# A gated recurrence with a soft mixture of experts: PSUM banks shared by need, filler transposes, wide roots and a new order of work

## The chip, the cores and the metric

The kernel runs on one core of a Trainium2 chip. Its engines are TensorE (PE, with its weight loads PEld), VectorE (DVE), ScalarE (ACT) and GpSimd (POOL); SyncE (SP) issues the DMAs. The metric is the device time of one execution in microseconds. A profiled execution lists the span from its first to its last instruction as well.

## The reference

The inputs are x, r_gate and i_gate of shape 4 x 5056 x 256, a_param of 256, phi of 256 x 32, and two weight arrays for eight experts.

```python
log_a = 8.0 * sigmoid(r_gate) * np.log(np.clip(sigmoid(a_param), 1e-6, 1 - 1e-6))
a_t = np.exp(log_a)
norm = np.sqrt(np.maximum(1.0 - a_t * a_t, 1e-6))
x_gated = norm * sigmoid(i_gate) * x
for t in range(S):
    h = a_t[:, t] * h + x_gated[:, t]
    y[:, t] = h
# y becomes 20224 x 256
logits = y @ phi                                   # 20224 x 32
d = softmax over the 20224 tokens of logits
slot_input = d.T @ y                               # 8 experts x 4 slots x 256
slot_out[e] = np.maximum(slot_input[e] @ w1[e], 0) @ w2[e]
c = softmax over the 32 slots of logits
out = c @ slot_out
```

Nothing can be written before all tokens have been read, because d is a softmax over tokens. So the kernel has a first part (recurrence, logits and the running weighted sum), a middle (the experts on 32 slots) and a last part (the second softmax and the output).

## The kernel before, in words

**Tiling.** 512 tokens are a quad (QT); there are 40, the last with 256 tokens. Units (UNITS) are quad 0 alone, then pairs of quads, then quad 39 alone: 21 units. Chunks (CHUNKS) are two units each, ten of them, and a last chunk of one. The 256 features are two halves h of 128. Tokens lie along the free dimension for the scan, so r and the gated x are transposed on TensorE, 128 x 128 at a time, and y is transposed back.

**One quad or unit passes these tasks** (the names are the planner's). TR (line 451) transposes a quad of r into PSUM, and SR (461, ACT) takes the tanh of half of it, which stands for the sigmoid. EX (492, ACT) makes a from it, per unit and half; SQ (503, POOL) squares a into a buffer N. SI (473, ACT) is the sigmoid of i, U (481, POOL) multiplies it with x, both in the natural layout. RT (516, ACT) is the root of 1 - a*a in N. TU (533, PE) transposes U's result into PSUM, ST (547, DVE) multiplies it with the root, SC (564, DVE) is the scan, which writes h over a in the buffer A. TY (584, PE) transposes h back and YC (598 on ACT, 600 on DVE) copies it from PSUM to yn.

**One group of four quads** passes LG (636, PE, logits), LE (649, DVE, with the running maximum), LD (665, POOL), TE (680, PE, transposes), ES (690, ACT, exponential), AC (710, PE, the weighted sum) and AE (726, DVE). After the last group come the merge of the partial sums (852 to 882), L1 (908), HS (922), HT (930), HR (936) and L2 (947) of the experts, and the table for the output (966 to 980). The last part has, per group, CT, CM, CS, CE, RR, CN, CH and CL (1014 to 1052), then HP (1079), HE (1090, 1092), OT (1102), OE (1114, 1116) and the store (1126).

**What sets the order.** Every engine runs its instructions in one fixed order, which a planner in the file works out while the kernel is built. It simulates the five engines from tasks with durations, latencies, dependences, buffers and priorities; at each free moment an engine takes the ready task with the lowest priority number whose buffers are free. ACT differs: its tanh, exponential, sigmoid and root tasks follow a written sequence (act_seq, lines 760 to 801), because a switch between the tables of the functions is an instruction of its own. Each chunk has three phases: tanh and exponentials, sigmoids, roots. PRE quads of the next chunk have their tanh in the sigmoid phase (PRE0 for chunk 0). The loads on SP follow the same sequence: r at each SR, i and x at each SI. A task without a table (a copy) may go ahead of the sequence only if its priority number is below that of the next one by more than ALAG (pick_act, line 246). DVE is asked before ACT when both could take a task.

**Buffers.** In SBUF: st (loaded tiles; 12), A (7), N (4), yn (7). In PSUM, eight banks of 512 floats per partition: rp (one pair of banks, for TR), up (two pairs, for TU; TR may use them as well, SHARE = 1), ms (two single banks). Single banks hold everything else; the halves of rp (tr) may serve as singles after the last tanh, and those of up (tu) after the last scan (tag_after, line 802). A pair for TU is held from TU until the end of SC.

The weights of the experts are loaded into st, A and N buffers as these come free (lines 808 to 836).

Of the kernel before, what the change touches and what calls it, by code (L numbers as in the profile page):

```python
# [15 lines left out]
P = 128  # L16
J = 4
# [7 lines left out]
PRE0 = 2  # L25
YLAG = 3

ALAG = 100
FILL = False
TRP = 2  # L30
# [3 lines left out]
SHARE = 1  # L34
G0 = 1
GM = 1
N_ST = 12
N_A = 7
N_N = 4
# [3 lines left out]
LOAD = 1.283  # L43
# [39 lines left out]
class Planner:  # L83
    def __init__(self, slots):
        self.tasks = []
        self.slots = {t: list(range(n)) for t, n in slots.items()}
        self.act_seq = []

        self.tag_after = {}
# [12 lines left out]
    def run(self):  # L102
# [41 lines left out]
        def begin(t, e):  # L144
            nonlocal n
            for b in t.alloc:
                b.tag = self.tag_for(b)
                b.slot = [self.slots[b.tag].pop(0) for _ in range(b.need.get(b.tag, 1))]
# [13 lines left out]
            for x in t.eng:  # L162
                ready[x].remove(t)
# [6 lines left out]
        while n_done < len(self.tasks):  # L170
# [4 lines left out]
            while finish and finish[0][0] <= now + 1e-9:  # L175
                _, _, t = heapq.heappop(finish)
                n_done += 1
                for b in [*t.alloc, *t.uses]:
                    b.users -= 1
                    if b.users == 0:  # L180
                        self.slots[b.tag] += b.slot
                for o in outs[id(t)]:
# [5 lines left out]
            while again:  # L188
                again = False
                for e in ("DVE", "ACT", "PE", "POOL", "SP"):  # L190
# [31 lines left out]
                    elif cands:  # L222
                        t = min(cands, key=lambda t: t.prio)
                        begin(t, e)
                        again = True
        self.end = now
        return order

    def tag_for(self, b, taken={}):
        for g in b.tags:  # L230
            if any(x.end is None or x.end > self.now + 1e-9 for x in self.tag_after.get(g, ())):
                continue
            if g == "tr" and not self.slots["rp"]:
                continue
            if b.late is not None and not b.late(self, g):
                continue
            if len(self.slots[g]) - taken.get(g, 0) >= b.need.get(g, 1):
                return g
        return None

# [28 lines left out]
def kernel(  # L269
# [37 lines left out]
    def plen(p):  # L307
# [5 lines left out]
         "rp": 1, "up": 2, "ms": 2, "tu": 4, "tr": 2, "hs": 4, "rm": 2, "hT": 2, "bd": 1}  # L313
    )
    T = {}
    if tc is not None:
# [91 lines left out]

    def load(nm, q):
# [13 lines left out]
        ld[(nm, q)] = add("SP", f"D{nm}{q}", 1.30 * n / J, prio=q, emit=emit, alloc=[b])  # L423
# [17 lines left out]
    def mk_sr(q):  # L441
# [3 lines left out]
        rp = Buf(("rp", "up") if SHARE & 1 else "rp", f"rp{q}")  # L445
# [11 lines left out]
        tr = add("PE", f"TR{q}", 0.245 * n, deps=[ld[("r", q)], t_const], prio=q - TRP, emit=e_tr,  # L457
# [28 lines left out]
    def mk_ex(p):  # L486
        c = plen(p)
        for h in range(H):
# [7 lines left out]
            EX[(p, h)] = add("ACT", f"EX{p}.{h}", 0.2 + 0.935 * c / 1024,  # L496
# [13 lines left out]
    def mk_rt(p):  # L510
        c = plen(p)
        for h in range(H):

            def e_rt(h=h):
                v = t(Nb[p])[:, h, :c]
                nc.scalar.activation(v, v, AF.Sqrt, bias=1.0, scale=-1.0)  # L516

            RT[(p, h)] = add("ACT", f"RT{p}.{h}", 0.1 + 0.85 * c / 1024, deps=[SQ[(p, h)]],
                             prio=pos_u(p), emit=e_rt, uses=[Nb[p]], kind="sqrt")

    def mk_scan(p):
        c = plen(p)
        tok0 = quads(p)[0] * QT
        for h in range(H):
            up = Buf(("up", "rp") if SHARE & 2 else "up", f"up{p}.{h}")
            up.late = lambda pl, tag: tag == "up" or SR[NQ - 1].start is None
# [12 lines left out]
            tu = add("PE", f"TU{p}.{h}", 0.123 * c / P, deps=[U[q] for q in quads(p)], prio=pos_u(p) - 20 + h * 0.1,  # L539
# [11 lines left out]
            ST[(p, h)] = add("DVE", f"ST{p}.{h}", 0.06 + 1.065 * c / 1024, deps=[tu, RT[(p, h)]],  # L551
# [21 lines left out]
    def mk_y(q):  # L573
        p, i = unit[q]
        YC[q] = []
        for b0 in range(0, qlen(q) // P, 2):
            yp = Buf(("ms", "tr", "tu"), f"yp{q}.{b0}")
# [24 lines left out]
            yc = add(("DVE", "ACT"), f"YC{q}.{b0}", 0.60 * nb / 2, deps=[ty], prio=q + (YLAG if q < NQ - YEND else 0),  # L602
# [11 lines left out]
    def mk_group(g):  # L614
# [8 lines left out]
        lp = Buf(("ms", "tr", "tu"), f"lp{g}")  # L623
        lD = Buf("lD", f"lD{g}")
        eS = Buf("eS", f"eS{g}")
        ep = Buf(("ms", "tr", "tu"), f"ep{g}")
        acc = Buf(("ms", "tr", "tu"), f"acc{g}")
# [3 lines left out]
        for h in range(H):  # L631

            def e_lg(h=h):
                for j, (q, o, _) in enumerate(segs):
# [8 lines left out]
                     prio=pos - 4 + fin, emit=e_lg, alloc=[] if h else [lp],  # L643
# [61 lines left out]
        for b in range(nb):  # L705

            def e_ac(b=b):
                for j, (q, o, _) in enumerate(segs):
# [10 lines left out]
                     prio=pos - 30 + fin, emit=e_ac, alloc=[] if b else [acc],  # L719
# [445 lines left out]
```

## Time and profile before

| | us |
|---|---|
| median of 3 runs | 337.19 (336.81 to 338.89) |
| the profiled execution | 339.49 |
| its span | 337.7 |
| mean granted TensorE clock over the span | 0.913 |
| HBM read / written | 78.94 MB / 20.71 MB |

The profile gives the busy time of each engine, the same by stretches of the span, groups of instructions by source line, and each engine's instructions in order of time. A row of a stretch has: its limits, its length, busy microseconds of PE, PEld, DVE, ACT and POOL with the count of instructions, the granted clock as a share of full speed, the DMA share and GB/s. A row of the timeline has start, length, engine, line, operation, output<-input, shape and count; several like instructions in a row stand as one row, and the bracket says how long the engine idled before it and what released it. A group has, after the first bar, busy us and mean ns of one instruction, and after the second the idle time before them.

### The profile page before, as it was taken

Reading aid. Unit: us, or ns where it says so; the run is one execution under the profiler, and the core shown is the slowest. Engines: PE = TensorE matmul, PEld = TensorE weight load, DVE = VectorE, ACT = ScalarE, POOL = GpSimd, SP = SyncE. Lnnn points to the kernel's source line nnn. Section 1 sums busy time; section 2 is a strip of 40 time slices with the busy share of each in tenths; the row PEclk is TensorE's granted clock in tenths of the full one; section 3 lists DMA queues with packets and bytes.
Section 4 is the critical chain, followed back from the end, with each engine's and each line's share of the span. In section 5 each row is a group of like instructions: output and inputs, shape, how many; then the busy total and the mean of one; then the engine's idle time right before and its main releaser. Section 6 shows DMA issues by size and latency. Waiting matters only on the chain. (4 is left out here: it accounts for less than half of the span.)

```text
span 337.7 us, 5590 instructions
## 1 busy us (share of the span) xinstructions
PE 266.9 (79%) x2032; PEld 187.3 (55%) x2032; DVE 259.7 (77%) x336; ACT 259.9 (77%) x306; POOL 198.9 (59%) x143
## 2 busy tenths in 40 slices
PE   4467639768789597895986969888889989979981
PEld 3357525644656456564664645754545567656761
DVE  0118847986979999789799999999833599898661
ACT  5977999989989999999799999995200049857650
POOL 4464687969949789698597978942010063375000
PEclk9755958978979999599899999799999999999997
DMA  7999876795876988869688796897995007979996
GB/s 240 416 411 378 284 265 233 276 352 207 328 291 234 364 296 293 304 229 358 222 309 323 268 338 202 310 403 282 376 387 202 3 1 305 397 297 380 406 400 274
DMA packets 30556, 100.02 MB, mean 296 GB/s; under 512 B 3648, under 2 KB 3648, under 8 KB 30528
## 3 DMA queue, kind: packets, MB, share of 16 engines
q1 hardware_dynamic: 29984, 99.63, 79.8%
q8 instruction: 16, 0.26, 0.3%
q10 hardware_dynamic: 544, 0.03, 0.1%
q14 instruction: 12, 0.10, 0.1%
HBM read 78.94 MB, written 20.71 MB: 295 GB/s over the span
## 5 line engine op out<-in xcount | busy, mean ns | idle before, releaser
L503 POOL TENSOR_TENSOR N<-A 128x1024 f32<-128x1024 f32 (+1 forms) x40 | 72.8, 1831 | 49.7 <-ACT A L492 49.4
L481 POOL TENSOR_TENSOR st<-st,st 128x1024 f32<-128x1024 f32 (+1 forms) x39 | 90.7, 2352 | 2.2 <-ACT st L473 2.2
L564 DVE TENSOR_TENSOR_SCAN A<-A,A,up 128x1024 f32<-128x1024 f32 (+4 forms) x40 | 82.2, 2060 | 2.0
L533 PE MATMUL up<-ident,st 128*128 128x128 f32 x316 | 50.6, 312 | 27.0 <-DVE A L564 23.5
L547 DVE SCALAR_TENSOR_TENSOR up<-N,up 128x1024 f32<-128x1024 f32 (+2 forms) x42 | 48.6, 1161 | 29.3 <-PE up L533 14.5
L533 PEld LDWEIGHTS up<-ident,st 128*128 128x128 f32 x316 | 40.7, 160 | 40.5 <-DVE A L564 19.3
L584 PE MATMUL ms<-ident,A 128*128 128x128 f32 x296 | 43.8, 285 | 10.4 <-DVE yn L600 8.9
L492 ACT ACTIVATE A<-A,ca 128x1024 f32<-128x1024 f32 (+2 forms) x42 | 48.9, 1184 | 0.5
L600 DVE COPY yn<-ms 128x512 f32<-128x512 f32 x67 | 43.3, 678 | 2.6 <-PE ms L584 2.5
L584 PEld LDWEIGHTS ms<-ident,A 128*128 128x128 f32 x296 | 33.6, 144 | 20.0 <-DVE yn L600 14.8
L473 ACT ACTIVATE st<-st 128x1024 f32<-128x1024 f32 (+1 forms) x40 | 39.6, 1037 | 0.1
L516 ACT ACTIVATE N<-N 128x1024 f32<-128x1024 f32 (+2 forms) x42 | 38.9, 995 | 0.1
L451 PE MATMUL rp<-ident,st 128*128 128x128 f32 x172 | 28.1, 315 | 12.9 <-DMA st<-in_r_gate_dram 9.4
L451 PEld LDWEIGHTS rp<-ident,st 128*128 128x128 f32 x172 | 23.3, 164 | 19.2 <-issue 5.7
L1045 POOL TENSOR_TENSOR lS<-lS,rs_all 128x512 f32<-128x512 f32 (+2 forms) x11 | 10.6, 962 | 31.9 <-DVE rs_all L1037 26.2
L1102 PE MATMUL ms<-bd,hT 128*128 128x512 f32 x88 | 27.8, 420 | 2.0 <-DVE st L1116 0.8
L461 ACT ACTIVATE A<-rp 128x1024 f32<-128x1024 f32 (+1 forms) x22 | 21.7, 987 | 5.0 <-PE rp L451 5.0
L710 PE MATMUL ms<-yn,eS 128*32 128x257 f32 x284 | 24.6, 396 | 0.4 <-ACT eS L690 0.4
L1031 ACT ACTIVATE lS<-lS 128x512 f32<-128x512 f32 (+2 forms) x11 | 6.4, 589 | 23.9 <-DVE lS L1028 23.6
L451 PE MATMUL up<-ident,st 128*128 128x128 f32 x144 | 20.2, 287 | 5.6 <-DVE A L564 4.9
L1114 ACT COPY st<-ms 128x512 f32<-128x512 f32 x28 | 16.3, 591 | 10.0 <-PE ms L1102 9.2
L636 PE MATMUL ms<-A,phi_sb 128*32 128x512 f32 x136 | 22.8, 700 | 0.3 <-ACT yn L598 0.3
(133 smaller groups left out, 397.5 us busy)
## 6 DMA issues: line engine op xcount, KB each, us to landing
st<-in_i_gate_dram SPq DMA_DIRECT2D x39, 512.0 KB, 5.3
st<-in_x_dram SPq DMA_DIRECT2D x39, 512.0 KB, 5.2
st<-in_r_gate_dram SPq DMA_DIRECT2D x38, 512.0 KB, 4.9
out_dram<-st SPq DMA_DIRECT2D x38, 512.0 KB, 3.6
A<-in_moe_w_dram SPq DMA_DIRECT2D x16, 512.0 KB, 5.6
st<-in_moe_w_dram SPq DMA_DIRECT2D x10, 512.0 KB, 6.1
N<-in_moe_w_dram SPq DMA_DIRECT2D x6, 512.0 KB, 7.8
st<-in_r_gate_dram SPq DMA_DIRECT2D x3, 256.0 KB, 3.2
```

Of the source, the lines that this page charges most:

```text
L451: nc.tensor.transpose(out=o[:, m, :], in_=t(st[("r", q)])[:, m * D + h * P : m * D + (h + 1) * P], identity=ident,)
L473: nc.scalar.activation(v, v, AF.Sigmoid)
L481: eng.tensor_tensor(out=v, in0=t(st[("i", q)])[:, : n * D], in1=v, op=ALU.mult)
L492: nc.scalar.activation(v, v, AF.Exp, scale=ca[:, h : h + 1], bias=ca[:, h : h + 1])
L503: eng.tensor_tensor(out=t(Nb[p])[:, h, :c], in0=v, in1=v, op=ALU.mult)
L516: nc.scalar.activation(v, v, AF.Sqrt, bias=1.0, scale=-1.0)
L533: nc.tensor.transpose(out=o[:, m, :], in_=t(st[("x", q)])[:, m * D + h * P : m * D + (h + 1) * P], identity=ident,)
L547: nc.vector.scalar_tensor_tensor(v, t(Nb[p])[:, h, :c], 1e-3, v, op0=ALU.max, op1=ALU.mult)
L564: nc.vector.tensor_tensor_scan(dst, dst, flat()[:, s0:s1], init, op0=ALU.mult, op1=ALU.add)
L584: nc.tensor.transpose(out=t(yp)[:, b * D + h * P : b * D + (h + 1) * P], in_=t(A[p])[:, h, o : o + P], identity=ident,)
L600: nc.vector.tensor_copy(out=dst, in_=v)
L1102: nc.tensor.matmul(t(op), t(hT)[:, b * P // 2 : (b + 2) * P // 2], T["bd"][part].rearrange("p i d -> p (i d)"), start=(part == 0), stop=(p ...
```

## The change

1. PSUM. The tags rp, up, ms, tu and tr are gone. All eight banks are four pairs (tag pair) whose halves are singles (tag one). TR and TU take a pair, at most RPM = 2 for r and UPM = 2 for x at a time. Everything else takes a single: first the free half of a pair already broken, else a half of the highest free pair, as long as fewer than ONEP = 3 pairs are broken (4 after the last scan has begun).
2. Filler. From 4 to 60 us of the plan, where TensorE has no task that can run, at least three banks are free and one has been free for over 1 us, two transposes of the identity into that bank are put in.
3. Roots. For the second unit of every chunk (WIDE) one ACTIVATE over both halves takes the place of two.
4. Order. No tanh of chunk 1 in chunk 0's sigmoid phase (PRE0 2 to 0). Priorities: TR at q - 10 (was q - 2), TU at pos - 28 (was - 20), LG at pos - 10 (was - 4), TY at q + 8 (was q + 2), YC at q + 7 (was q + 3). ALAG 100 to 0. A few assumed durations and latencies of the planner are changed.
5. Buffers: st 12 to 10, A 7 to 9, N 4 to 3; the bytes are the same.

```diff
-PRE0 = 2
-YLAG = 3
-ALAG = 100
+PRE0 = 0
+YLAG = 9
+ALAG = 0
-TRP = 2
+TRP = 10
-SHARE = 1
-G0 = 1
+RPM = 2
+UPM = 2
+ONEP = 3
+WARMT = 60.0
+QL = 99
+TUP = 28
+ACP = 30
+LGP = 10
+YCP = -2
+WD = 1
+G0 = 2
-N_ST = 12
-N_A = 7
-N_N = 4
+N_ST = 10
+N_A = 9
+N_N = 3
-LOAD = 1.283
+LOAD = 1.41
...
-            lat = {"PE": 0.25, "ACT": 0.1, "DVE": 0.1, "POOL": 0.12, "SP": 2.0}[eng[0]]
+            lat = {"PE": 0.25, "ACT": 0.13, "DVE": 0.13, "POOL": 0.12, "SP": 2.6}[eng[0]]
...
+                    elif e == "PE" and self.warm is not None and self.warm_from <= now < self.warm_to:
+                        t = self.filler(now)
+                        if t is not None:
+                            begin(t, e)
...
+            if g == "pair":
+                k = b.name[:2]
+                if self.pairs_of.get(k, 0) < self.pair_max.get(k, 4) and any(
+                    {2 * i, 2 * i + 1} <= self.banks for i in range(4)
+                ):
+                    return g
+            elif g == "one":
+                if self.pick_one() is not None:
+                    return g
...
+    def pick_one(self):
+
+        half = [i for i in self.banks if i ^ 1 not in self.banks and i // 2 in self.broken]
+        if half:
+            return min(half)
+        whole = [i for i in range(3, -1, -1) if {2 * i, 2 * i + 1} <= self.banks]
+        if whole and len(self.broken) < self.one_pairs():
+            return 2 * whole[0]
+        return None
+
+    def filler(self, now):
+
+        free = [i for i in self.banks if now - self.since.get(i, -1e9) > 1.0]
+        if len(self.banks) < 3 or not free:
+            return None
+        i = min(free, key=lambda i: self.since.get(i, -1e9))
+        return Task(("PE",), "WU", 0.22, 0.2, (), 1e9, lambda: self.warm(i), alloc=[self.fixed(i)], kind="warm", shape="T")
...
-        make("rp", 1, [P, 2, QT], ps)
-        make("up", 2, [P, 2, QT], ps)
-        make("ms", 2, [P, QT], ps)
+        make("pair", 4, [P, 2, QT], ps)
-        T["tu"] = [T["up"][i // 2][:, i % 2, :] for i in range(4)]
-        T["tr"] = [T["rp"][0][:, i, :] for i in range(2)]
+        T["one"] = [T["pair"][i // 2][:, i % 2, :] for i in range(8)]
...
+    WIDE = {p for ch in chunks for p in ch[WD:]} if WD is not None else set()
...
-        rp = Buf(("rp", "up") if SHARE & 1 else "rp", f"rp{q}")
+        rp = Buf("pair", f"rp{q}")
...
-        for h in range(H):
+        wide = p in WIDE
+        for h in range(1 if wide else H):
 
             def e_rt(h=h):
-                v = t(Nb[p])[:, h, :c]
+                v = t(Nb[p])[:, :, :c] if wide else t(Nb[p])[:, h, :c]
                 nc.scalar.activation(v, v, AF.Sqrt, bias=1.0, scale=-1.0)
...
-            up = Buf(("up", "rp") if SHARE & 2 else "up", f"up{p}.{h}")
-            up.late = lambda pl, tag: tag == "up" or SR[NQ - 1].start is None
+            up = Buf("pair", f"up{p}.{h}")
...
-            yp = Buf(("ms", "tr", "tu"), f"yp{q}.{b0}")
+            yp = Buf("one", f"yp{q}.{b0}")
...
-            yc = add(("DVE", "ACT"), f"YC{q}.{b0}", 0.60 * nb / 2, deps=[ty], prio=q + (YLAG if q < NQ - YEND else 0),
+            yc = add(("DVE", "ACT"), f"YC{q}.{b0}", 0.60 * nb / 2, deps=[ty], prio=q + YCP + (YLAG if q < NQ - YEND else 0),
...
+    def e_warm(i):
+        for _ in range(2):
+            nc.tensor.transpose(out=T["one"][i][:, :P], in_=ident, identity=ident)
+
+    planner.warm, planner.warm_from, planner.warm_to = e_warm, 4.0, WARMT
+    planner.pair_max = {"rp": RPM, "up": UPM}
+    planner.one_pairs = lambda: ONEP if SC[(NP - 1, H - 1)].start is None else 4
```

More of the change, by code (lines that the diff above doesn't have):

```diff
@@ L146, in begin @@
             for b in t.alloc:
[L147 to L148 removed]
+                self.take(b)
             dur = t.alt.get(e, t.dur)
@@ new lines, in give @@
+    def give(self, b):
+        if b.tag == "pair":
+            i = b.slot[0]
+            self.banks |= {2 * i, 2 * i + 1}
+            self.since[2 * i] = self.since[2 * i + 1] = self.now
+            self.pairs_of[b.name[:2]] -= 1
+        elif b.tag == "one":
+            i = b.slot[0]
+            self.banks.add(i)
+            self.since[i] = self.now
+            if i ^ 1 in self.banks:
+                self.broken.discard(i // 2)
+        else:
+            self.slots[b.tag] += b.slot
@@ L762, with roots @@
     ahead = []
+    def roots(k):
+        return [("RT", p, h) for p in chunks[k] for h in range(1 if p in WIDE else H)]
     for k in range(NC):
@@ L776 @@
             phases.append([("SR", q) for q in ahead])
-        phases.append([("RT", p, h) for p in chunks[k] for h in range(H)])
+        if k >= QL and k > 0:
+            phases.append(roots(k - 1) if k > QL else [])
+        if k < QL or k == NC - 1:
+            phases.append(roots(k))
     for ph in phases:
```

95 lines of the change are left out of this document (61 added, 34 removed).

## The prediction

> **What bounds the kernel now.** I read the page first, then busy time by stretches of the span, then the ScalarE instructions in order of time, then who released each pause.
>
> ```profile
> span 337.7 us, 5590 instructions
> ...
> PE 266.9 (79%) x2032; PEld 187.3 (55%) x2032; DVE 259.7 (77%) x336; ACT 259.9 (77%) x306; POOL 198.9 (59%) x143
> ```
> ```profile
> 0.00:20.00 20.00, 9.04 (x41) 7.67 (x42) 3.50 (x7) 14.96 (x16) 9.60 (x33) 0.83 0.90 340
> 20.00:40.00 20.00, 14.86 (x86) 13.44 (x85) 12.94 (x12) 15.72 (x16) 9.95 (x6) 0.66 0.97 361
> ...
> 180.00:200.00 20.00, 16.01 (x145) 11.39 (x145) 19.22 (x21) 19.86 (x22) 17.13 (x9) 1.00 0.84 299
> ```
> ```profile
> 200.00:226.00 26.00, 21.51 (x192) 15.38 (x196) 24.79 (x24) 25.81 (x29) 20.49 (x13) 0.93 0.82 302
> 226.00:241.00 15.00, 12.96 (x111) 7.21 (x104) 14.68 (x19) 6.93 (x14) 2.44 (x2) 1.00 0.90 330
> ...
> 251.00:277.00 26.00, 25.15 (x318) 15.56 (x306) 15.08 (x38) 3.54 (x7) 5.12 (x5) 1.00 0.27 101
> 277.00:332.00 55.00, 50.35 (x235) 34.78 (x235) 45.90 (x87) 36.84 (x68) 18.40 (x18) 1.00 0.90 356
> ```
>
> The averages (ACT and DVE 77%, PE 79%) hide four stages. In a stretch the columns after the length are PE, PEld, DVE, ACT, POOL, then granted clock, DMA share and GB/s. Up to 226 us ACT is the bound: 19.86 of 20 us in the steady part, with DVE close behind at 19.22. From 226 to 241 DVE finishes the scans (14.68 of 15). From 251 to 277 the expert layers run on PE (25.15 of 26), and then the output runs on PE too (50.35 of 55) with the DMA at 0.90. So what is won before 226 moves everything behind it, unless DVE is late; what is won on PE before 226 counts only where ACT waits for it.
>
> ACT's own timeline shows its pace and where it pauses (start, length, and in brackets the pause before):
>
> ```profile
> 14.31 1.28 ACT L473 ACT_TABLE_LOAD   x1
> ...
> 21.91 1.02 ACT L461 ACTIVATE A<-rp 128x1024 f32<-128x1024 f32 x1 [2.44 <-PE rp L451]
> ...
> 24.25 3.04 ACT L516 ACTIVATE N<-N 128x512 f32<-128x512 f32 x4
> 27.31 1.28 ACT L492 ACT_TABLE_LOAD   x1
> ...
> 34.13 1.02 ACT L461 ACTIVATE A<-rp 128x1024 f32<-128x1024 f32 x1 [2.25 <-PE rp L451]
> ...
> 37.58 1.28 ACT L473 ACT_TABLE_LOAD   x1
> ...
> 45.91 3.90 ACT L516 ACTIVATE N<-N 128x1024 f32<-128x1024 f32 x4
> ...
> 74.63 0.60 ACT L690 ACTIVATE eS<-ms 128x512 f32<-128x512 f32 x1 [1.20 <-PE ms L680]
> ...
> 96.98 0.60 ACT L690 ACTIVATE eS<-ms 128x512 f32<-128x512 f32 x1 [1.41 <-PE ms L680]
> ...
> 129.91 1.28 ACT L516 ACT_TABLE_LOAD   x1
> ...
> 145.00 2.01 ACT L473 ACTIVATE st<-st 128x1024 f32<-128x1024 f32 x2
> ...
> 150.74 1.28 ACT L516 ACT_TABLE_LOAD   x1
> ...
> 162.95 0.60 ACT L690 ACTIVATE eS<-ms 128x512 f32<-128x512 f32 x1 [2.22 <-PE ms L680]
> ...
> 173.92 1.28 ACT L516 ACT_TABLE_LOAD   x1
> ```
>
> From one load of the root table to the next an undisturbed chunk takes 150.74 - 129.91 = 20.83 us; the one with the 2.22 us pause takes 23.18. The pauses that can be removed are few: 2.44 and 2.25 us at the start, for the transposed r tiles (L451), and 1.20 + 1.41 + 2.22 = 4.83 us later, where the exponentials of a group (L690) wait for their transposes (L680). Apart from the waits for the first loads, the rest is ACT's own work.
>
> **Part by part: the start (PRE0 = 0).** Two tanh of chunk 1 (L461) leave the sigmoid phase of chunk 0, and their two r loads move behind i2 and x2. Before, this phase held both, with the 2.44 us wait. After, I rebuild it from the rows: sigmoid table at 14.31 as now (1.28 each table), three sigmoids in 2.95, root table, the roots in 3.04 less 0.10: chunk 0 is through at about 22.8 instead of 27.31. Chunk 1's exponential phase now lasts 37.58 - 27.31 = 10.27, minus the 2.25 us wait (its r tiles are transposed while ACT does the roots), plus two tanh at 0.95: 9.9. It ends at 32.7 instead of 37.6. The gain is 4.7 us, the two waits; the moved tanh only change place. Cover: 23 tiles of 512 KB must be in for chunk 1, 12.06 MB; at 340 GB/s and then 361 (rows above) that takes 34.6 us, and the last sigmoid needs its tile at about 37.8. So it fits with some 3 us, and nothing beyond it. Ends: 1.5 (loads late) and 4.7; I take 4.0, as the first two rates are measured with the same queue.
>
> **The second unit's root in one instruction.** The two sizes of root, and a chunk's last squares on POOL:
>
> ```profile
> L516 ACT ACTIVATE N<-N 128x1024 f32<-128x1024 f32 x38 | 37.1, 1046 | 0.1
> ...
> L516 ACT ACTIVATE N<-N 128x512 f32<-128x512 f32 x2 | 1.2, 622 | 0.0
> ```
> ```profile
> 142.63 3.75 POOL L503 TENSOR_TENSOR N<-A 128x1024 f32<-128x1024 f32 x2 [0.77 <-ACT A L492]
> ```
>
> Four roots in a row take 3.90 us (row at 45.91); one alone takes 1.046, so each further one adds 0.951. From 512 to 1024 elements the mean grows from 622 to 1046 ns, 0.848 us per 1024:
>
> One start-up less saves 0.951 - 0.848 = 0.10 us; ten chunks, 1.0 us on the bounding engine. It now waits for both squares of POOL and gives DVE its first half 0.85 us later. Both are covered: the squares end at 142.63 + 3.75 = 146.4, the root runs after 152, and DVE has about 7 us of the first unit's scans before it. Without that cover, 0.85 per chunk.
>
> **PSUM by pairs or singly, and TensorE's new order.** Now r's transposes borrow the banks of the scans, and the queue stands behind a transpose that waits for a scan:
>
> ```profile
> 160.09 1.97 PE L533 MATMUL up<-ident,st 128*128 128x128 f32 x8 [1.60 <-DVE A L564]
> 161.85 1.06 PE L680 MATMUL ms<-ident,lD 128*128 128x128 f32 x4
> ```
>
> That is the 2.22 us pause: L680 is queued behind L533, which waited 1.60 for a scan. UPM = 2 leaves as many scan pairs as now, so this order can come back; but r has two pairs of its own, and logits come forward (LGP). No row prices the new order. Bounds: 0 and 4.83 us of these pauses; I take half, 2.4.
>
> **Filler transposes up to 60 us.** What eight transposes cost at a low and at a full clock stands in a stretch where TensorE did nothing else:
>
> ```profile
> 30.91 1.91 PE L584 MATMUL ms<-ident,A 128*128 128x128 f32 x8
> ...
> 35.21 1.09 PE L451 MATMUL rp<-ident,st 128*128 128x128 f32 x8 [1.11 <-ACT A L461]
> ```
>
> A filler is two transposes: with 8 in 1.09 to 1.97, it takes 0.27 to 0.49 us. It goes where the plan has PE idle, so at worst it stands before a real transpose: with the 11 tanh inputs of that time, up to 5.4 us lost if all are hit, 0 if none. It may raise the clock (0.66 in 20:40): a tanh input's 8 transposes would take 1.09 rather than 1.91, but the two waits this could shorten are already counted. I take -0.3.
>
> Here eight transposes went from 1.91 to 1.09 us within 5 us. The Trainium skill, page "TensorE: Matmul & The Clock Gate", section "Part 4: PE-mode transpose", says the opposite: the full clock does not engage for transpose mode. By that page the fillers would only cost; these rows disagree with it, and by them fillers can warm. As the benefit is counted at nothing, the sum is the same less at most 0.3.
>
> **Copies of y (ALAG 0, YLAG 9, YCP -2).** One copy on either engine:
>
> ```profile
> L600 DVE COPY yn<-ms 128x512 f32<-128x512 f32 x67 | 43.3, 678 | 2.6 <-PE ms L584 2.5
> ...
> L598 ACT COPY yn<-ms 128x512 f32<-128x512 f32 x7 | 3.9, 583 | 3.7 <-PE ms L584 3.7
> ```
>
> A copy that lies some 7 quads behind ACT's next instruction may now go ahead of it on ACT. On DVE it costs 678 ns, on ACT 583, of which 0.10 overlaps as with the roots, so 0.48 us. Before the last root every such copy lengthens the bound; after it, ACT is idle (6.93 of 15) and it is free. Scans now go ahead of copies, so copies do fall behind. Ends 0 and 30 copies (three a chunk); I take 2, -1.0. At the end this order helps: DVE did copies ahead of the last full chunk's first scan product, whose transposes had ended before:
>
> ```profile
> 216.82 2.40 PE L533 MATMUL up<-ident,st 128*128 128x128 f32 x16
> ```
> ```profile
> 220.31 1.22 DVE L547 SCALAR_TENSOR_TENSOR up<-N,up 128x1024 f32<-128x1024 f32 x1
> ```
>
> The transposes of both halves ended at 216.82 + 2.40 = 219.2, the first half at about 218, so scans could start up to 2.3 us earlier. The copies come back later, partly on ACT. Ends -2 and +2.3; I take +1.0.
>
> **Buffers.** Issues of loads, the use of one, and the time to landing:
>
> ```profile
> 123.33 0.37 SPq L421 DMA_DIRECT2D st<-in_i_gate_dram  x1
> ...
> 138.61 7.54 SPq L421 DMA_DIRECT2D st<-in_r_gate_dram  x3
> ```
> ```profile
> 148.47 1.09 PE L451 MATMUL up<-ident,st 128*128 128x128 f32 x8 [0.39 <-DVE A L564]
> ```
> ```profile
> st<-in_r_gate_dram SPq DMA_DIRECT2D x38, 512.0 KB, 4.9
> ```
>
> st 12 to 10: the sigmoid at 145.00 uses the tile issued at 123.33, and r issued at 138.61 is transposed at 148.47. Twelve tiles a chunk make 1.74 us a tile, so two slots less means loads 3.5 us later. Landing takes 4.9 us. So r keeps 9.9 - 4.9 - 3.5 = 1.5 us, i far more. N 4 to 3: the second unit's square must now wait for the root product of the unit two before:
>
> ```profile
> 204.02 1.23 DVE L547 SCALAR_TENSOR_TENSOR up<-N,up 128x1024 f32<-128x1024 f32 x1
> ```
> ```profile
> 207.00 3.75 POOL L503 TENSOR_TENSOR N<-A 128x1024 f32<-128x1024 f32 x2 [0.29 <-ACT A L492]
> ```
>
> Margin 207.00 - 205.25 = 1.75 us, and behind it POOL's products for x. A from 7 to 9 pays for later copies. I take 0 for all three, with up to 1 us a chunk lost if the margins go. G0 changes nothing at GM = 1. The tail after 241 has the same eight banks and engines at work; 0, within 2 either way.
>
> **Sum.** 4.0 + 1.0 + 2.4 - 0.3 - 1.0 + 1.0 = 7.1 us. The profiled execution took 339.49 us (337.7 span and 1.8 around it) and would take 332.4; the median shown is 337.19, so I predict **330.1**.
>
> **Rivals.** (a) *Only the start and the roots pay*: the group pauses return, since L680 still stands behind a waiting scan transpose, and copies and fillers cost their 1.3; end order 0. 4.0 + 1.0 - 1.3 = 3.7 gained: 333.5. For it: the cap of two scan pairs; against: r's own pairs.
> (b) *Loads bind*: with ten slots and r 1.5 us from being late, r waits appear; 0.5 us a chunk over ten eats 5.0: 335.1. For it: DMA share 0.97 in 20:40; against: 299 GB/s suffices later. The Trainium skill's page "DMA: Bandwidth & Descriptors", section "Specifications", puts a core's HBM limit near 358 GB/s; the rows' 361 is no less.
> (c) *Slower: copies on ACT.* DVE is full with 19.22 of 20, scans go first, and ACT takes three copies a chunk: 30 x 0.48 = 14.4 lost against 8.1 gained: 343.5. It decides from 17 copies before the last root on. For it: the copy goes before ACT's own next instruction; against: the 7 quads are nearly two chunks, which a copy seldom waits.
> (d) *More*: all pauses vanish, 4.7 + 1.0 + 4.8 + 2.3 and the tail 2: 14.8, 322.4.
> That sharing banks changes nothing is inside (a).
>
> **How the numbers follow.** Forecast 0.42 (326 to 333), (a) 0.18, (b) 0.15, (c) 0.13, (d) 0.12. A measurement tells about 1% (3.4 us) from no change, so faster means under 333.8: the forecast, (d), and two thirds of (a): 0.66. Same: (b), the rest of (a), the mild end of (c): 0.22. Slower 0.12. The range 322.5 to 338.5 leaves out the far half of (d) and most of (c).
>
> **What would show it.** Right: ACT's exponential table load for chunk 1 near 23 and the sigmoid load near 33; the 42 root instructions become 32, wide ones of about 1.9 us; the L680 pauses halved; chunk pace 20.7. Wrong: more than 17 copies on ACT before its last root; new pauses of ACT behind DMA or of POOL's squares behind DVE; first output later than 273 us.

## The result and the profile after

The changed kernel takes 365.16 us (median of 4 runs, 364.08 to 365.99) against 337.0 for the kernel before (4 runs, 332.88 to 338.89): a ratio of 1.0878, 95% interval 1.0775 to 1.0982. I had forecast 330.1 with an upper end of 338.5, so the sign is wrong and the time lies far above that. Medians in this text are of all executions, ratios leave out the slow ones (some per cent longer at a lower granted clock), and the profile of e10 is of a slow one.

The head of the page after, and the busy time by stretches of its stages (columns as in the prediction: length, PE, PEld, DVE, ACT, POOL, granted clock, DMA share, GB/s):

```profile
span 363.8 us, 5797 instructions
...
PE 280.8 (77%) x2132; PEld 196.7 (54%) x2132; DVE 258.4 (71%) x333; ACT 259.4 (71%) x299; POOL 198.7 (55%) x143
```
```profile
60.00:220.00 160.00, 129.15 (x1054) 93.24 (x1055) 143.54 (x147) 147.18 (x144) 126.69 (x66) 0.90 0.78 282
...
228.00:242.00 14.00, 11.40 (x106) 5.75 (x98) 10.66 (x15) 6.36 (x13) 2.44 (x2) 1.00 0.92 323
242.00:253.00 11.00, 8.55 (x71) 4.34 (x69) 6.23 (x17) 1.41 (x4) 1.05 (x2) 1.00 0.87 327
253.00:283.00 30.00, 25.20 (x315) 14.65 (x316) 13.10 (x34) 2.83 (x7) 4.64 (x4) 1.00 0.33 122
283.00:360.00 77.00, 57.52 (x231) 37.52 (x230) 41.83 (x83) 38.50 (x72) 18.63 (x18) 0.93 0.65 259
```

Read the last row against that of before, where 277 to 332 had PE at 50.35 of 55 and the DMA at 0.90. Now the output takes 77 us, PE is idle for 19 of them and the DMA is at 0.65: nothing is full. Where no engine is full and work remains, the time goes into waits between the engines.

Dates from the timelines of the profiled executions place the loss (us):

| | before | after | longer by |
|---|---|---|---|
| last root of the chunks ends | 226.5 | 228.3 | 1.8 |
| last scan ends (from there) | 241.0 (14.5) | 241.7 (13.3) | -1.2 |
| first expert's first matmul | 250.6 (9.6) | 253.1 (11.5) | 1.8 |
| first output matmul | 277.2 (26.5) | 282.8 (29.7) | 3.2 |
| end of the span | 337.7 (60.6) | 363.8 (81.0) | 20.4 |

The steps are summed to 26.0 of 26.1 us. Almost all of it lies behind the last scan, where I had put 0.

**The start came out as forecast.** ScalarE's timeline (start, length):

```profile
14.35 1.28 ACT L557 ACT_TABLE_LOAD   x1
...
18.61 1.28 ACT L601 ACT_TABLE_LOAD   x1
...
22.87 1.28 ACT L545 ACT_TABLE_LOAD   x1
...
32.94 1.28 ACT L557 ACT_TABLE_LOAD   x1
```

The exponential table of chunk 1 comes at 22.87 (forecast 22.8) and its sigmoid table at 32.94 (32.7). **So did the roots**, in ScalarE's groups by shape:

```profile
L601 ACT ACTIVATE N<-N 128x2048 f32<-128x2048 f32 x10 | 19.0, 1896 | 0.0
L601 ACT ACTIVATE N<-N 128x1024 f32<-128x1024 f32 x18 | 18.1, 1052 | 0.1
```

Ten wide ones of 1.896 us, 32 in all with the four short ones. **The group pauses did not.** ScalarE's groups in 60 to 220 us:

```profile
L775 ACT ACTIVATE eS<-pair 128x512 f32<-128x512 f32 x7 | 4.2, 597 | 11.4 <-PE pair L765 11.4
```

11.4 us of pauses against the 4.83 counted in the prediction. One of them, from all engines in order of time:

```profile
107.51 2.35 DVE L632 SCALAR_TENSOR_TENSOR pair<-N,pair 128x1024 f32<-128x1024 f32 x2
...
109.77 4.58 DVE L649 TENSOR_TENSOR_SCAN A<-A,A,pair 128x1024 f32<-128x1024 f32 x2
...
112.26 1.94 PE L618 MATMUL pair<-ident,st 128*128 128x128 f32 x8 [3.52 <-DVE A L649]
...
114.12 1.94 PE L721 MATMUL pair<-A,phi_sb 128*32 128x512 f32 x8
...
115.99 1.12 PE L765 MATMUL pair<-ident,lD 128*128 128x128 f32 x4
...
117.14 0.60 ACT L775 ACTIVATE eS<-pair 128x512 f32<-128x512 f32 x1 [2.99 <-PE pair L765]
```

TensorE stands 3.52 us at the state transposes L618 until the first scan, which ran behind two state products, has freed a pair. The logits L721 and the group's transposes L765 queue behind it, and ScalarE's exponential is 2.99 us late.

**The output is a chain through the halves of a pair.** All engines in order of time, from the middle of the output (matmuls L1200; the copies of a block on DVE, L1214, and on ACT, L1212):

```profile
341.49 1.19 PE L1200 MATMUL pair<-bd,hT 128*128 128x512 f32 x4 [0.48 <-ACT st L1212]
...
342.72 0.69 DVE L1214 COPY st<-pair 128x512 f32<-128x512 f32 x1 [0.98 <-PE pair L1200]
...
343.44 0.58 ACT L1212 COPY st<-pair 128x512 f32<-128x512 f32 x1 [1.03 <-DVE st L1214]
344.08 1.20 PE L1200 MATMUL pair<-bd,hT 128*128 128x512 f32 x4 [0.90 <-ACT st L1212]
```

PE fills both halves of a pair, DVE copies one half, ACT copies the other only when DVE has done, PE goes on only when ACT has done: 344.08 - 341.49 = 2.59 us for these two blocks, and of the three steps on them no two overlap. The waits in 283 to 360 us (total, times, longest) show the same:

```profile
PEld pair L1200 <- ACT st L1212: 15.4, 15, 1.9
...
ACT st L1212 <- DVE st L1214: 11.6, 10, 2.2
...
DVE st L1214 <- ACT st L1212: 9.4, 7, 2.0
```

Before, in 277 to 332 us, no copy of the output waits for another copy; the largest row of ACT there is

```profile
ACT st L1114 <- PE ms L1102: 9.2, 13, 2.7
```

A copy on ACT has no data from a copy on DVE; they read different banks. What they share is the tile: four tiles of two banks replaced the earlier ones, and a half is a slice of such a tile.

### The profile page after: what moved, and what is told of

Same layout as the page of the kernel before. It is cut to its first block, busy times and chain, and to the rows that moved or that the text cites. A ratio compares the mean times of both kernels' runs of the same rounds, so it can differ in the third digit from the quotient of the medians.

```text
span 363.8 us, 5797 instructions
## 1 busy us (share of the span) xinstructions
PE 280.8 (77%) x2132; PEld 196.7 (54%) x2132; DVE 258.4 (71%) x333; ACT 259.4 (71%) x299; POOL 198.7 (55%) x143
## 5 line engine op out<-in xcount | busy, mean ns | idle before, releaser
L649 DVE TENSOR_TENSOR_SCAN A<-A,A,pair 128x1024 f32<-128x1024 f32 (+4 forms) x40 | 81.6, 2058 | 0.5
L618 PE MATMUL pair<-ident,st 128*128 128x128 f32 x316 | 50.3, 317 | 32.3 <-DVE A L649 31.1
L1200 PE MATMUL pair<-bd,hT 128*128 128x512 f32 x158 | 50.3, 447 | 19.3 <-ACT st L1212 9.5
L618 PEld LDWEIGHTS pair<-ident,st 128*128 128x128 f32 x316 | 43.8, 167 | 38.2 <-issue 31.5
L632 DVE SCALAR_TENSOR_TENSOR pair<-N,pair 128x1024 f32<-128x1024 f32 (+2 forms) x42 | 47.7, 1158 | 12.4 <-ACT N L601 8.8
L1212 ACT COPY st<-pair 128x512 f32<-128x512 f32 x52 | 29.4, 587 | 37.2 <-PE pair L1200 16.0
L685 DVE COPY yn<-pair 128x512 f32<-128x512 f32 x73 | 46.5, 685 | 12.9 <-PE pair L669 12.5
L535 PE MATMUL pair<-ident,st 128*128 128x128 f32 x316 | 43.8, 284 | 6.5 <-DMA st<-in_r_gate_dram 5.2
L669 PE MATMUL pair<-ident,A 128*128 128x128 f32 x316 | 43.2, 279 | 6.7 <-DVE yn L685 2.5
L1200 PEld LDWEIGHTS pair<-bd,hT 128*128 128x128 f32 x158 | 29.0, 203 | 35.9 <-ACT st L1212 15.4
L669 PEld LDWEIGHTS pair<-ident,A 128*128 128x128 f32 x316 | 34.1, 141 | 17.7 <-issue 6.2
L535 PEld LDWEIGHTS pair<-ident,st 128*128 128x128 f32 x316 | 36.0, 145 | 12.9 <-issue 5.2
L545 ACT ACTIVATE A<-pair 128x1024 f32<-128x1024 f32 (+1 forms) x40 | 39.8, 998 | 0.9 <-PE pair L535 0.7
L601 ACT ACTIVATE N<-N 128x1024 f32<-128x1024 f32 (+3 forms) x32 | 38.0, 1249 | 0.1
L1214 DVE COPY st<-pair 128x512 f32<-128x512 f32 x27 | 18.6, 691 | 23.0 <-PE pair L1200 13.4
L721 PE MATMUL pair<-A,phi_sb 128*32 128x512 f32 (+1 forms) x164 | 27.4, 713 | 0.7 <-DVE accS L811 0.7
```

The costliest lines, as they stand in the source:

```text
L535: nc.tensor.transpose(out=o[:, m, :], in_=t(st[("r", q)])[:, m * D + h * P : m * D + (h + 1) * P], identity=ident,)
L545: nc.scalar.activation(t(A[p])[:, :, i * QT : i * QT + c], t(rp)[:, :, :c], AF.Tanh, scale=0.5)
L618: nc.tensor.transpose(out=o[:, m, :], in_=t(st[("x", q)])[:, m * D + h * P : m * D + (h + 1) * P], identity=ident,)
L632: nc.vector.scalar_tensor_tensor(v, t(Nb[p])[:, h, :c], 1e-3, v, op0=ALU.max, op1=ALU.mult)
L649: nc.vector.tensor_tensor_scan(dst, dst, flat()[:, s0:s1], init, op0=ALU.mult, op1=ALU.add)
L669: nc.tensor.transpose(out=t(yp)[:, b * D + h * P : b * D + (h + 1) * P], in_=t(A[p])[:, h, o : o + P], identity=ident,)
```

## The experiments

Theory A: the two halves of a pair tile wait for each other, since waits are set for a tile as a whole. Theory B: the rule that picks a bank takes one just freed, so no slack is left. For the chunks C to E came later. In the table, *pauses* is the sum of the waits ahead of the group's exponential on ScalarE over the whole timeline, the next two columns are dates in the profiled execution, the last one is a length, and the ratio is to the kernel before on the same chip.

| run | median us | ratio, interval | pauses | last root | first expert | from there to the end |
|---|---|---|---|---|---|---|
| before | 334.4 to 337.0 | | 6.2 | 226.5 | 250.6 | 87.1 |
| after | 365.2 | 1.088, 1.078 to 1.098 | 14.6 | 228.3 | 253.1 | 110.7 |
| e1 | 337.1 | 1.005, 1.002 to 1.009 | 15.1 | 230.3 | 254.9 | 82.5 |
| e2 | 344.5 | 1.025, 1.019 to 1.032 | 15.6 | 229.0 | 252.3 | 91.7 |
| e3 | 335.3 | 0.996, 0.991 to 1.001 | 3.2 | 222.2 | 246.4 | 87.1 |
| e4 | 334.5 | 0.995, 0.991 to 1.000 | 1.8 | 218.2 | 242.3 | 88.8 |
| e5 | 335.6 | 1.003, 1.000 to 1.007 | 15.6 | 229.7 | 253.1 | 82.3 |
| e6 | 334.3 | 0.998, 0.994 to 1.001 | 9.4 | 227.9 | 250.5 | 82.4 |
| e7 | 337.2 | 1.010, 1.006 to 1.014 | 15.2 | 228.2 | 252.8 | 82.3 |
| e8 | 332.2 | 0.992, 0.987 to 0.997 | 2.8 | 220.0 | 246.4 | 83.9 |
| e9 | 340.7 | 1.014, 1.003 to 1.024 | 15.5 | 230.2 | 255.0 | 82.3 |
| e10 | 341.1 | 1.009, 1.000 to 1.017 | 15.5 | 232.9 | 255.5 | 84.3 |
| e11 | 333.6 | 0.993, 0.988 to 0.997 | 5.0 | 223.0 | 247.3 | 86.4 |
| e12 | 330.6 | 0.989, 0.979 to 0.999 | 2.6 | 220.1 | 246.9 | 82.0 |
| e13 | 336.7 | 1.004, 1.000 to 1.008 | 4.3 | 229.6 | 254.4 | 82.5 |
| e14 | 337.7 | 1.004, 1.000 to 1.007 | 3.4 | 231.0 | 253.6 | 84.0 |
| e15 | 333.6 | 0.994, 0.990 to 0.999 | 2.3 | 217.9 | 247.0 | 83.6 |

**e1: eight single tiles in the tail.** The plan, the order and the choice of banks are the changed kernel's; only the tiles are other ones.

```diff
+    def retile():
+            psc.__exit__(None, None, None)
+            ps2 = ctx.enter_context(tc.tile_pool(name="ps2", bufs=1, space=bass.MemoryType.PSUM))
+            T["one"] = [ps2.tile([P, QT], F32, name=f"o{i}", tag=f"o{i}", bufs=1) for i in range(8)]
...
+            if task.name == "L1.0":
+                retile()
```

> The changed kernel with one thing different: from the experts' first matmuls on, the eight banks are eight tiles of their own in place of four pairs; the plan, the order of all engines and the choice of banks stay. Theory A (the two halves of a pair tile wait for each other, because waits are set per tile) expects that the part from the experts on shrinks from 110.7 us (253.1 to 363.8) to about 87, as before (250.6 to 337.7), so about 342 us. Theory B (the pick of a bank just freed leaves no slack; tiles don't matter) expects no change, 365 within 2.

337.06 us: 28 us come back. The ratio falls from 1.088 to 1.005, so 0.5% is left of the loss, and the part from the first expert on is 4.6 us shorter than before's (82.5 against 87.1). The bank number that the plan gives each instruction is the changed kernel's; only what waits for what is new. Busy time in its output, and its waits in the same stretch:

```profile
279.00:330.00 51.00, 48.48 (x231) 35.35 (x231) 44.52 (x84) 38.04 (x73) 19.09 (x18) 1.00 0.94 372
```
```profile
ACT st L1213 <- PE o L1201: 10.1, 23, 1.5
DVE st L1215 <- PE o L1201: 4.7, 16, 0.5
PEld o L1201 <- ACT st L1213: 3.9, 14, 0.9
```

PE is at 48.48 of 51 again, the copies wait for PE alone and no longer for each other, and the waits of PE's weight loads for the copies on ACT fell from 15.4 to 3.9. Theory A held. Why a copy that only reads a tile waits for another reader of it isn't shown.

**e2: pairs kept, the free bank that has been free longest.**

```diff
     def pick_one(self):
+        if self.one_pairs() == 4:
+            return min(self.banks, key=lambda i: self.since.get(i, -1e9), default=None)
```

> The changed kernel, but from the last scan on a single bank is the one that has been free longest, over all four pairs, in place of the free half of a broken pair; the tiles stay pairs, the planned order of work is the same. Theory B (packing into two pairs) expects most of the 23 us back, about 343 us. Theory A expects part of it at most, since the halves of a tile still wait for each other though they come up in turn less often: 350 to 360.

344.5: the part from the first expert on falls from 110.7 to 91.7. This is near B's 343 and below the 350 to 360 that A expected, so A had the share of the rule too small: the changed rule packs neighbours in time into one pair. With the better rule the shared tiles still cost 9.2 us against e1 (91.7 and 82.5). **e5 puts both together** (e1 with e2's rule):

> The changed kernel with both remedies: eight single tiles from the first expert on, and of the free banks the one that has been free longest. Theory A (the two halves of one pair tile wait for each other) expects what the eight tiles alone gave, 337 us within 2, and the part from the first expert's first matmul to the end at 82 to 84 us against 82.5, since the choice of bank costs only what the shared tile makes of it. Theory B (a bank that has just been freed leaves no slack) expects 2 us or more on top: 335 or less, with that part at 80 or less. The main part is the changed kernel's, so the last root should end at 228 to 231 us in either.

335.6, and 82.3 us for that part against 82.5 in e1, as A expected. With single tiles the rule is worth nothing that shows: B acts only through A. **e3: single tiles in the tail of the kernel before**, where halves of earlier pairs lent themselves too:

> The kernel before, with eight tiles of their own from the experts' first matmuls on; plan and order are the same. In it six of the eight single banks are halves of rp and up. Theory A expects a gain here too, smaller, since two banks are tiles of their own and the free banks take turns: 2 to 6 us, about 333. Theory B expects 337, no change.

335.3, a ratio whose interval holds 1, and the same 87.1 us: before, the shared tiles cost nothing that can be told, and the 2 to 6 us that A expected did not come. Up to the first expert e3 runs the instructions of before in the same order, and yet its profile has 3.2 us of pauses where that of before has 6.2, and its last root ends 4.3 us earlier. Dates of single profiles are uncertain by that much.

**e4: the start alone** (before, with `PRE0 = 0`):

> The kernel before with PRE0 = 0 alone. The prediction's first term expects the two waits of 2.44 and 2.25 us gone and the exponential table of chunk 1 loaded near 23 us: 4 us less, 333. The rival (what the start gains is lost again at the group pauses and at the end of the scans, which follow other things) expects 337.

334.5: 0.5% gained (0.0 to 0.9), between the two. Its profiled execution ends the last root 8.3 us earlier than that of before; 4.5 us of these are pauses that were shorter there, not the start. Against e3 it is 222.2 - 218.2 = 4.0 us.

**e6: state product, scan, state product, scan.** Theory C: the group pauses come from VectorE's order ST, ST, SC, SC (the rows at 107.51 and 109.77).

```diff
... (from one line)
-deps=[tu, RT.get((p, h), RT[(p, 0)])],
+deps=[tu, RT.get((p, h), RT[(p, 0)])], lat=0.0,
...
```

> The changed kernel with eight single tiles in the tail, and with one number of the plan changed in the chunks: the latency that the planner gives the state products on VectorE is 0, so that it puts state product, scan, state product, scan in its order in place of two state products and then two scans. Theory C (the group pauses of 11.4 us on ScalarE in the changed kernel come from that order on VectorE: a pair of banks is held for a second state product longer, and the logits and the transposes of the weights queue behind it on TensorE) expects the pauses back at 3 to 6 us, the last root at 220 to 224 us where it was 230, and 329 to 332 us in all. Its rival (the pauses come from the sharing of the pairs itself in the chunks: transposes, logits and weights wait for the other half of a pair, in whatever order VectorE works) expects pauses of 9 us or more and 335 to 338 us.

9.4 us of pauses, as the rival has it, and 334.3 us, between the two; 5.6 of the 15 us are gone. The counterpart of L618, here L619, still stands 2.6 us at a scan. Its rows on TensorE:

```profile
136.91 1.77 PE L619 MATMUL pair<-ident,st 128*128 128x128 f32 x8 [2.63 <-DVE A L650]
138.61 1.93 PE L722 MATMUL pair<-A,phi_sb 128*32 128x512 f32 x8
140.47 0.67 PE L766 MATMUL pair<-ident,lD 128*128 128x128 f32 x4
140.97 1.04 PE L619 MATMUL pair<-ident,st 128*128 128x128 f32 x8
141.94 0.64 PE L796 MATMUL pair<-yn,eS 128*32 128x257 f32 x8
142.40 1.04 PE L722 MATMUL pair<-A,phi_sb 128*32 128x512 f32 x8
```

**e7: no fillers.** The plan is kept, the transposes of the identity are not issued (they compute nothing that is used).

```diff
... (from one line)
-lambda: self.warm(i), alloc=[self.fixed(i)]
+lambda: None, alloc=[self.fixed(i)]
...
```

> The changed kernel with eight single tiles in the tail, planned as it is, but the transposes of the identity are left out (they compute nothing that the output needs). If they hold the granted clock of the first chunks up, as the profile of the changed kernel with 1.00 in the first slices suggests, their absence should lengthen the first transposes and move the exp table load of the second chunk from 22.9 to 23.7 us to 24 or later, and the whole by 0.5 to 2 us over 337. If they only keep TensorE busy beside work that waits for loads, the times stay within 1 us of 337, and the table load stays at 23 to 24 us.

337.2 us against 337.1 of e1; the intervals of their ratios overlap. The table load stands at 23.0 us. Of the first 20 us, the stretch of the changed kernel and then that of e7:

```profile
0.00:20.00 20.00, 15.58 (x118) 14.94 (x118) 3.50 (x7) 15.55 (x17) 9.54 (x33) 1.00 0.91 350
```
```profile
0.00:20.00 20.00, 8.27 (x36) 7.13 (x37) 3.50 (x7) 15.44 (x17) 9.46 (x33) 0.87 0.92 345
```

The granted clock does rise from 0.87 to 1.00 with the fillers, and ScalarE does as much work in both (15.55 and 15.44 us): faster transposes for its tanh did not get more work out of it. All 118 matmuls of the first row are transposes. Here the Trainium skill's page "TensorE: Matmul & The Clock Gate", section "Part 4: PE-mode transpose", by which transposes don't engage the full clock, disagrees with the clock of these rows.

**e9: the group's transposes ahead of the third state transposes.** Theory D: in the plan the two pairs of r and the two of the scans hold all eight banks at that moment; the tanh that frees a pair and then the group's transposes are put first, in six chunks.

```diff
+            move = [t for t in order[i:j] if t.name[:2] == "SR" and any(banks(b) & ep for b in t.uses)] + [order[j]]
+            rest = [t for t in order[i:j] if t not in move]
...
+                order[i : j + 1] = move + rest
```

> The changed kernel with eight single tiles in the tail, and in six chunks TensorE's transposes of the group (with the tanh on ScalarE that frees the bank for them) put ahead of the third state transposes; banks, priorities and all the rest as in e1. Theory D (the group pauses come from TensorE standing at the third state transposes until a scan has freed their pair, 2.6 to 3.6 us, with the group's transposes and the logits queued behind it, and from the two pairs of r and the two of the scans holding all eight banks at that moment) expects the pauses at 0 to 4 us in place of 15.1, the last root at 219 to 223 us in place of 230.3, and 327 to 331 us. Theory C alone (the order of state products and scans on VectorE) expects no change, 335.5 to 338.

D fell: 340.7 us, above what either expected, and 15.5 us of pauses. The trace shows why, and gave theory E:

```profile
136.07 0.66 PE L766 MATMUL pair<-ident,lD 128*128 128x128 f32 x4 [3.44 <-ACT A L546]
...
138.03 1.94 PE L722 MATMUL pair<-A,phi_sb 128*32 128x512 f32 x8
...
140.03 0.60 ACT L776 ACTIVATE eS<-pair 128x512 f32<-128x512 f32 x1 [1.79 <-PE pair L722]
```

The transposes were done at 136.73, but the exponential waits for the logits L722, which it doesn't read: in the plan the transposes stand in bank 1 and these logits in bank 0, the two halves of one pair. It is A again, in the chunks. **e10 joined e9 and e6:**

> e9 and e6 together: the group's transposes first, and state products and scans in turn on VectorE. If both causes are there and add up, the pauses are 0 to 2 us, the last root ends at 217 to 220 us and the whole takes 325 to 328. If the group's place is all of it, this is within 1.5 us of e9.

15.5 us of pauses, and a ratio of 1.009 (1.000 to 1.017) against e9's 1.014 (1.003 to 1.024): no gain over e9 that can be told.

**e13: the exponential ahead of the next logits too**, so that the program has no logits before it to wait for:

```diff
...
+            ahead(order, sr + [f"TE{g}"], f"TU{2 * g + 5}.0", [f"LD{g}"])
+            ahead(order, [f"ES{g}"], f"LG{g + 1}.0", [f"TE{g}"])
```

> e9 with one more step of the order written by hand: in the same six chunks the exponential of the group on ScalarE stands ahead of the next group's logits in the program (and so ahead of the tanh of the second r tile). Theory E (logits and the group's transposes stand in the two halves of one pair tile, so the exponential waits for the logits too if they come before it in the program: in e9 the transposes had ended at 136.73 us, the exponential began at 140.03, when the logits had ended) expects pauses of 0 to 3 us in place of 15.5, the last root at 218 to 222 us in place of 230.2, and 327 to 331 us in all. If the pause has another cause (ScalarE's own chain, VectorE's scans), the exponential only moves, another pause takes its place, and the last root stays at 228 to 231 us.

The pauses fall from 15.5 to 4.3 us, so E names what held the exponential. But the last root stays at 229.6 and the time is 336.7, as the other expectation has it: another pause takes the place. ScalarE's groups in 60 to 220 us:

```profile
L546 ACT ACTIVATE A<-pair 128x1024 f32<-128x1024 f32 (+1 forms) x28 | 27.9, 998 | 6.5 <-PE pair L536 6.4
...
L776 ACT ACTIVATE eS<-pair 128x512 f32<-128x512 f32 x7 | 4.1, 581 | 1.1 <-PE pair L766 1.1
...
L684 ACT COPY yn<-pair 128x512 f32<-128x512 f32 x1 | 0.6, 585 | 3.6 <-PE pair L670 3.6
```

The wait has moved: 6.4 us for r's transposes and 3.6 for one of y's. **e14, e13 with VectorE in turn as in e6:**

> e13 with state products and scans in turn on VectorE as in e6, so that the third state product's pair comes free a state product's time (1.2 us) earlier. Theory E alone expects this within 1.5 us of e13; if VectorE's order is a cause of its own, 2 us or more below it.

337.7, within the 1.5 us of E: VectorE's order gives nothing on top of e13.

**The other parts without the sharing.** e8 is the kernel before with the start, the wide roots and single tiles in the tail; e11 the same without the wide roots; e12 is e11 with four of the plan's new costs: the latency after ACT and DVE 0.13 us (was 0.10), that of every load, not of the weights alone, 2.6 (was 2.0), the sums and reciprocals RR of the output 0.7 (was 0.35, both plus a part by size), the expert transposes HT 0.33 (was 0.24). e15 has the start, the wide roots, the single tiles and these costs.

> The kernel before with three parts alone: the start without early preparation (as in e4), the roots of a second unit in one instruction, and eight single tiles from the first expert on (as in e3); none of the sharing of banks, of the fillers and of the new costs and priorities. If the parts add up, this is 334.7 less 0.4 to 1.6 for the start, 0.4 to 1.2 for the tiles and 0.5 to 1 for the roots: 331 to 333.5 us, with the last root at 216 to 218 us. If the part from the first expert on takes back whatever the chunks give, as it did in e4, it stays at 334 to 335.

> The kernel before with the new start and with eight single tiles from the first expert on, without the wide roots of e8. If the wide roots save their 0.10 us in ten chunks, this is 0.5 to 1.5 us over e8's 332.2; if their later first half costs VectorE more than that, it is below 332: the last scan of e8 ended 16.9 us behind the last root, that of the kernel before 14.5, which speaks for 330 to 332.

> e11 with the changed kernel's new costs in the plan as well (latencies 0.13 us, loads of the weights 2.6, the first products of the combination 0.7, the transposes of the experts 0.33). If these costs order the tail better, as the changed kernel's tail on eight tiles (82.4 us from the first expert to the end, against 87.1 of before) suggests, the part from the first expert on is at 82 to 84 us and the whole at 327 to 330. If that tail comes from the sharing of banks in the combination and not from the costs, it stays within 1.5 us of e11.

> The kernel before with the new start, the wide roots, eight single tiles from the first expert on and the new costs (e8 and e12 together). e8 was 0.8% and e12 1.1% under the kernel before; the wide roots take 0 to 1 us off e12: 329 to 331 us, a ratio of 0.983 to 0.990.

332.2, 333.6, 330.6 and 333.6 us. e8 came within its range, though its last root (220.0) is later than expected. e8 and e11 cannot be told apart, so the wide roots' 1 us is below what shows. e12 has the lowest median, with a ratio of 0.989 from four executions and an interval (0.979 to 0.999) that holds the ratios of e8, e11 and e15. Its tail is as short as expected (82.0 us; e11 86.4); but e8 has 83.9 without the new costs and e15 83.6 with them, so that the costs order the tail better is not shown. e15 lies 2.6 us over its range: its chunks are the shortest (last root 217.9), but 13.5 us pass from the last scan, at 233.5, to the first expert. In e15 the chunks' pauses in 60 to 220 us are:

```profile
L695 ACT ACTIVATE eS<-ms 128x512 f32<-128x512 f32 x7 | 4.1, 581 | 0.9 <-PE ms L685 0.9
```

It has the roots, the start and four of the costs of the changed kernel, without its sharing of banks, its fillers and its new priorities and buffers: 0.9 us in place of 11.4. With the banks as before this number is 0.3 to 4.9 us (e4 0.3, e12 1.6, e8 1.7, e3 1.8, e11 3.6, before 4.9).

## Why the prediction was wrong

The step that failed is "The tail after 241 has the same eight banks and engines at work; 0, within 2 either way." The banks and engines are the same; the tiles are not, and the tail cost 23.6 us more from the first expert on. I had the new tiles before me in the diff (four pairs, and singles as slices of them) and priced bank capacity only, not what is waited for. e1 shows the cause: tiles of one bank from there on, with nothing else changed, shorten this part from 110.7 to 82.5 us. e2 shows the other half: with shared tiles, 19.0 us of it hang on the rule that fills the two halves of one pair one after the other. The prediction priced neither.

Point by point:

- *Start*: right. Chunk 1's root table moved from 44.61 to 39.97, 4.6 us; I took 4.0.
- *Roots*: right in size, three of a chunk 3.81 us against four in 3.90, 0.09 a chunk.
- *Group pauses, 2.4 gained*: wrong sign. Ahead of the last root they grew from 4.8 to 11.4 us, 6.6 lost, more than the start and the roots gained. The 4.83 us were not all there to win either: they are one execution's, and e3 with the same chunks has 1.8. The reasoning of rival (a), that L680 still stands behind a waiting scan transpose, was right about the place; it put the loss at none beyond today's pauses.
- *Fillers, 0.3 lost*: not contradicted, but below what e7 can tell.
- *Copies on ACT, 1.0 lost*: right in kind. One copy of 0.58 us lies ahead of the last root (two taken); rival (c), which needed 17, is out, though the sign it stood for came.
- *End order, 1.0 gained*: right, 14.5 to 13.3 us from last root to last scan, 1.2.
- *Buffers, 0*: no run separates them. POOL's squares waited longer for ACT, and nothing shows whether N's three buffers have a part.
- *Rival (b), loads*: out. The DMA share in 60 to 220 us fell from 0.81 to 0.78, and ScalarE waited for PE.

**What stays open** is the chunks. Shown: the exponential waits for logits in the other half of its pair (e9, e13); undoing that moves the wait to r's transposes and the time stays; with the banks as before the pauses are 0.3 to 4.9 us in the same stretch, with the changed kernel's banks and order 11.4 (after) and 11.9 (e1). Not shown: how much is the shared pairs, how much that r's two and the scans' two hold all eight banks with TensorE in order, and how much the new priorities and buffers. The 1.8 us more from the last scan to the first expert stand in e1 too (11.5 us as in the changed kernel, 9.6 before), and no run explains them. Eight single tiles weren't tried in the chunks, since one instruction there reads 1024 elements across two banks.

## What to carry to other kernels

When a change cuts several buffers out of one tile, ask of every reader and writer which others it will now wait for that touch another slice; the capacity can stay the same and the overlap go. In a profile this looks like a stage in which no engine and no queue is near full, with two copies naming each other as releaser though neither has the other's data. A pause that a queue produces need not be gone when the order in the queue is changed, as e9 and e13 showed: look for who stands at the head next.

## What the runs showed of the hardware

A wait of TensorE can cost more than its length. In e6's rows above, after 2.63 us of waiting eight transposes took 1.77 us and eight logit matmuls 1.93; the same groups at 140.97 and 142.40 took 1.04 each. The granted clock goes with it: 1.00 from 130.00 to 134.28 us, 0.56 from 136.90 to 138.60, 0.50 from 138.60 to 140.50, and 1.00 again from 140.97. In the changed kernel's rows at 112.26 to 115.99, at a granted clock of 0.50, three groups took 1.94, 1.94 and 1.12 us; by e6's 1.04, 1.04 and 0.67 that is 2.25 us of the 2.99 us pause (worked out, not tried).

The length of the wait alone does not decide it. In the kernel before, TensorE waits 1.60 to 1.64 us for a scan ahead of the third state transposes of each chunk from 60 to 220 us. The eight transposes behind it took 1.97 us three times, as in the prediction's row at 160.09 (granted clock 0.50 from 160.09 to 162.90), 1.59 once, and 1.09 three times, as here (1.00 from 116.50 to 119.00):

```profile
116.56 1.09 PE L533 MATMUL up<-ident,st 128*128 128x128 f32 x8 [1.60 <-DVE A L564]
```

All three pauses that the prediction counts as 4.83 us come behind groups of 1.97 or 1.59 us, and none behind one of 1.09 (the one of 1.97 at 136.61 has no pause behind it). So the queue behind a waiting transpose, which the prediction names as their cause, is not enough by itself. In the changed kernel the eight transposes took 1.06 us after waits of 3.12 and 3.37 us, and 1.94 after five of 3.52 to 3.56; pauses of 0.97 and 1.15 us came there behind the groups of 1.06 us too. The Trainium skill's page "TensorE: Matmul & The Clock Gate", section "HAM oscillation — how this bites in real kernels", tells of a halved clock after gaps over some 3.4 us; here waits of 1.60 us were followed by one too, so a shorter wait can be enough.
